# x + alpha * fx on one core: the first load moves from the sync engine's queue to ScalarE's

## The chip, the cores and the metric

The kernel runs on one core of one Trainium2 chip. The metric is the time of one execution on the device in microseconds (us). Before the change the median of three runs is 150.9 us (150.83 to 150.96).

## The reference

Two bfloat16 tensors of shape 512 x 32 x 640 (20.97 MB each) and one bfloat16 scalar go in; one tensor of the same shape comes out.

```python
def reference(x, fx, alpha):
    return x + alpha * fx
```

So 41.94 MB are read from HBM, 20.97 MB are written, and each element needs one multiplication and one addition.

## The kernel before

Each tensor is seen as 128 rows, one for each SBUF partition, of 160 units; a unit (`K`) is 512 elements, or 1 KiB of a row. All data lies in one tile, `room`, of 128 partitions by 207 units (`ROOM`). A written plan, the string `PLAN`, sets the order of all steps, and a loop at the end of the kernel goes through it line by line. The order is kept as written (a manual schedule).

The lines of the plan are:

- `f a b @ at`, `x a b @ at`, `s a b @ at`: one transfer of units a to b of fx, of x or of the output, to or from place `at` of `room`. Each is one `dma_start` in `transfer` (line 96). The row of a transfer is (b - a) KiB long; `f 0 8` has rows of 8 KiB, `f 8 64` rows of 56 KiB, `x 0 64` rows of 64 KiB.
- `a`: `spread_alpha` loads alpha (line 86), and spreads it over the 128 partitions with a matmul against ones (line 90) and a copy to `a_f` (line 91).
- `m t n`: VectorE multiplies n units at place t by alpha, in place (line 110).
- `+ t u n`: VectorE adds the n units at place u to those at place t (line 115).

The plan begins so:

```python
f 0 8 @ 143
f 8 64 @ 151
a
x 0 64 @ 0
m 143 64
f 64 128 @ 79
+ 0 143 24
```

All transfers are issued by the sync engine (SP), on one queue. The first five (`f 0 8`, `f 8 64`, alpha, `x 0 64`, `f 64 128`) wait for nothing and are issued one behind the other at the start. The later loads (`x 64 88`, `x 88 104`, `x 104 128`, `f 128 160`, `x 128 160`) go into places that a multiplication or an addition must have left first, so SP waits for VectorE before it issues them. Then come the stores: `s 0 64` (issued after the addition `+ 192`), `s 64 128` and `s 128 160`. The first multiplication, `m 143 64`, needs both `f 0 8` and `f 8 64`, and alpha. At the end a `nop` on SP waits for all but the last store (line 122). ScalarE has no work of the kernel's at all.

Of the kernel before, what the change touches and what calls it, by code (L numbers as in the profile page):

```python
# [1 line left out]

# [4 lines left out]

ALU = mybir.AluOpType
F32 = mybir.dt.float32

K = 512
P = 128
ROOM = 207

PLAN = """
f 0 8 @ 143
f 8 64 @ 151
a
x 0 64 @ 0
# [3 lines that stand above are left out]
x 64 88 @ 143  # L33
+ 24 167 16
x 88 104 @ 167
+ 40 183 24
x 104 128 @ 183
m 79 64
+ 143 79 17
f 128 160 @ 64  # L40
+ 160 96 7
+ 167 103 16
+ 183 119 9
x 128 160 @ 96
m 64 32
+ 192 128 9
s 0 64 @ 0 after + 192
+ 201 137 6
s 64 128 @ 143
+ 96 64 32  # L50
s 128 160 @ 96
"""


@with_exitstack
def kernel(
    ctx: ExitStack,
    tc: tile.TileContext,
    x: bass.AP,
    fx: bass.AP,  # L60
    alpha: bass.AP,
    out: bass.AP,
):
    nc = tc.nc
    whole = {
        name: t.flatten_outer_dims().rearrange("(p n) d -> p (n d)", p=P)
        for name, t in (("x", x), ("f", fx), ("s", out))
    }
    assert whole["x"].shape[1] == 160 * K

    consts = ctx.enter_context(tc.tile_pool(name="consts", bufs=1))
    psum = ctx.enter_context(tc.tile_pool(name="psum", bufs=1, space=bass.MemoryType.PSUM))
    rooms = ctx.enter_context(tc.tile_pool(name="rooms", bufs=1))
    ctx.enter_context(tc.manual_schedule())

    room = rooms.tile([P, ROOM * K], x.dtype, name="room")
    a_f = consts.tile([P, 1], F32, name="a_f")
    info = mybir.DependencyInfo(mybir.DependencyClass.Sync, mybir.DependencyReason.DATA)
    done, moved = [], {}

    def units(t, a, b):
        return t[:, a * K : b * K]

    def spread_alpha():
        a_1 = consts.tile([1, 1], alpha.dtype, name="a_1")
        done.append(nc.sync.dma_start(out=a_1[:], in_=alpha[None, :]))  # L86
        ones = consts.tile([1, P], alpha.dtype, name="ones")
        nc.vector.memset(ones[:], 1.0)  # L88
        a_ps = psum.tile([P, 1], F32, name="a_ps")
        done.append(nc.tensor.matmul(a_ps[:], ones[:], a_1[:], start=True, stop=True))  # L90
        nc.vector.tensor_copy(out=a_f[:], in_=a_ps[:])  # L91

    def transfer(what, a, b, at, after):
        away, here = units(whole[what], a, b), units(room, at, at + b - a)
        out, in_ = (away, here) if what == "s" else (here, away)
        r = nc.sync.dma_start(out=out, in_=in_)  # L96
        if after:
            tc.add_manual_dep(r.ins, moved[after].ins.name, info, reason="issued late")
        moved[what, a] = r
        done.append(r)  # L100

    for step in PLAN.strip().split("\n"):
        what, *rest = step.split()
        if what == "a":
            spread_alpha()
        elif what == "m":
            t, n = map(int, rest)
            f = units(room, t, t + n)
            done.append(
                nc.vector.tensor_scalar(out=f, in0=f, scalar1=a_f[:], scalar2=None, op0=ALU.mult)  # L110
            )
        elif what == "+":
            t, u, n = map(int, rest)
            xt, f = units(room, t, t + n), units(room, u, u + n)
            moved[what, t] = nc.vector.tensor_tensor(out=xt, in0=xt, in1=f, op=ALU.add)  # L115
            done.append(moved[what, t])
        else:
            a, b, _, at = rest[:4]
            after = (rest[5], int(rest[6])) if len(rest) > 4 else None
            transfer(what, int(a), int(b), int(at), after)  # L120

    last = nc.sync.nop(nofuse=True)
    for i in done[:-1]:
        tc.add_manual_dep(last.ins, i.ins.name, info, reason="all but the last store")


# [1 line left out]
_INS = ['x', 'fx', 'alpha']  # L128
_OUTS = [((512, 32, 640), 'bfloat16')]


# [23 lines left out]
```

## Time and profile before

| quantity | value |
|---|---|
| median of three runs | 150.9 us (150.83 to 150.96) |
| time of the profiled execution | 150.81 us |
| its span | 149.0 us |
| VectorE busy | 65.9 us (44%) |
| DMA queue q1 (all transfers) | 62.92 MB, 98.1% of 16 engines' span |
| mean rate over the span | 422 GB/s |

The span runs from the first to the last instruction that the profiler saw on the core; some 1.8 us of the execution lie outside it. The share of the DMA queue is the time that its packets took, divided by the span of all 16 DMA engines. In this trace a packet of data is one row of a transfer on one DMA engine; each transfer of 128 rows gives each of the 16 engines 8 rows. A window's rate counts a row's bytes where the row begins, so narrow windows swing.

### The profile page before, as it was taken

The numbers are of one execution on the slowest core, as the hardware profiler recorded it, in microseconds if no ns is written. First come the engines' busy times: TensorE is split into PE (matmuls) and PEld (weight loads), VectorE is DVE, ScalarE is ACT, GpSimd is POOL, SyncE is SP. The second block draws the span as 40 slices with busy tenths as digits, with TensorE's granted clock in tenths as the row PEclk, the third lists the DMA queues.
The fourth block names the chain that finished last, engine by engine and source line by source line (L and its number), as shares of the span: only waits on it lengthen the run. The fifth ranks groups of instructions, "written<-read, shape, count | busy, mean of one in ns | idle before, by whom it ended". The sixth has DMA issues, their size and how long they took to land.

```text
span 149.0 us, 85 instructions
## 1 busy us (share of the span) xinstructions
PE 0.2 (0%) x1; PEld 0.1 (0%) x1; DVE 65.9 (44%) x15; POOL 0.2 (0%) x4
## 2 busy tenths in 40 slices
PE   0000000000000000000000000000000000000000
PEld 0000000000000000000000000000000000000000
DVE  0000009940089998699999307969910000000000
POOL 0000000000000000000000000000000000000000
DMA  5997996969899796999998999999696969697994
GB/s 183 592 400 339 493 528 281 563 281 563 369 475 528 317 563 281 416 429 391 462 449 387 422 431 449 449 501 545 299 563 281 563 281 563 281 563 308 457 449 194
DMA packets 1730, 62.92 MB, mean 422 GB/s; under 512 B 194, under 2 KB 194, under 8 KB 194
## 3 DMA queue, kind: packets, MB, share of 16 engines
q1 hardware_dynamic: 1730, 62.92, 98.1%
HBM read 41.94 MB, written 20.97 MB: 422 GB/s over the span
## 4 chain that ended last, share of the span: by engine, by line
DMA 38%; DVE 32%; another core or an unknown queue 1%; SPq 1%; issue 0%; DVEq 0%
DMA room<-in_x_dram 38%; DVE room L115 27%; DVE room L110 6%; SPq L96 1%; SPq L86 0%; DVEq L115 0%
## 5 line engine op out<-in xcount | busy, mean ns | idle before, releaser
L115 DVE TENSOR_TENSOR room<-room 128x12288 bf16<-128x12288 bf16 (+6 forms) x10 | 43.7, 4419 | 11.5 <-DMA room<-in_x_dram 11.5
L110 DVE TENSOR_SCALAR room<-room,a_f 128x32768 bf16<-128x32768 bf16 (+1 forms) x3 | 22.0, 7330 | 9.0 <-DMA room<-in_fx_dram 9.0
L91 DVE COPY a_f<-a_ps 128x1 f32<-128x1 f32 x1 | 0.2, 159 | 21.4 <-PE a_ps L90 21.4
L88 DVE MEMSET ones<- 1x128 bf16 x1 | 0.2, 165 | 0.8 <-PEq L139 0.8
L90 PE MATMUL a_ps<-a,ones 1*128 1x1 bf16 x1 | 0.2, 159 | 22.2 <-DMA a<-in_alpha_dram 22.2
L90 PEld LDWEIGHTS <-ones 1*128 1x128 bf16 x1 | 0.1, 101 | 1.0 <-DVE ones L88 1.0
L139 POOL MEMSET const-bfloat16-1.0<- 128x1 bf16 x1 | 0.1, 101 | 0.0
L139 POOL MEMSET const-uint8-127<- 128x1 uint8 x1 | 0.1, 101 | 0.0
L139 POOL MEMSET const-float32-0.0<- 128x1 f32 x1 | 0.1, 98 | 0.2 <-issue 0.2
L139 POOL MEMSET const-float32-1.0<- 128x1 f32 x1 | 0.1, 98 | 0.0
## 6 DMA issues: line engine op xcount, KB each, us to landing
room<-in_fx_dram SPq DMA_DIRECT2D x1, 7168.0 KB, 21.1
room<-in_x_dram SPq DMA_DIRECT2D x2, 3072.0 KB, 20.7
room<-in_fx_dram SPq DMA_DIRECT2D x1, 4096.0 KB, 15.7
room<-in_x_dram SPq DMA_DIRECT2D x1, 4096.0 KB, 16.7
out_dram<-room SPq DMA_DIRECT2D x1, 4096.0 KB, 39.5
room<-in_x_dram SPq DMA_DIRECT2D x1, 2048.0 KB, 20.5
room<-in_fx_dram SPq DMA_DIRECT2D x1, 1024.0 KB, 4.6
out_dram<-room SPq DMA_DIRECT2D x2, 39.7
```

The costliest lines, as they stand in the source:

```text
L88: nc.vector.memset(ones[:], 1.0)
L90: done.append(nc.tensor.matmul(a_ps[:], ones[:], a_1[:], start=True, stop=True))
L91: nc.vector.tensor_copy(out=a_f[:], in_=a_ps[:])
L96: r = nc.sync.dma_start(out=out, in_=in_)
L110: nc.vector.tensor_scalar(out=f, in0=f, scalar1=a_f[:], scalar2=None, op0=ALU.mult)
L115: moved[what, t] = nc.vector.tensor_tensor(out=xt, in0=xt, in1=f, op=ALU.add)
L139: nc = _bacc.Bacc("TRN2", target_bir_lowering=False, num_devices=1)
```

## The change

The first line of the plan gets the mark `by act`, and `transfer` issues a marked load on `nc.scalar` in place of `nc.sync`. It is still the first transfer in the program's order; place, rows and bytes are the same. On SP the list of transfers then begins with `f 8 64`. The way in which `after` is read is rewritten, and `spread_alpha` takes an argument; on the `a` line that list is empty, so alpha's load gets no wait by it.

```diff
-f 0 8 @ 143
+f 0 8 @ 143 by act
 f 8 64 @ 151
 a
 x 0 64 @ 0
...
-    def spread_alpha():
+    def late(r, after):
+        if after:
+            what, a = after[1], int(after[2])
+            tc.add_manual_dep(r.ins, moved[what, a].ins.name, info, reason="issued late")
+
+    def spread_alpha(after):
         a_1 = consts.tile([1, 1], alpha.dtype, name="a_1")
         done.append(nc.sync.dma_start(out=a_1[:], in_=alpha[None, :]))
+        late(done[-1], after)
...
-        r = nc.sync.dma_start(out=out, in_=in_)
-        if after:
-            tc.add_manual_dep(r.ins, moved[after].ins.name, info, reason="issued late")
+        queue = nc.scalar if after == ["by", "act"] else nc.sync
+        r = queue.dma_start(out=out, in_=in_)
+        if queue is nc.sync:
+            late(r, after)
...
-            spread_alpha()
+            spread_alpha(rest)
...
-            after = (rest[5], int(rest[6])) if len(rest) > 4 else None
-            transfer(what, int(a), int(b), int(at), after)
+            transfer(what, int(a), int(b), int(at), rest[4:])
```

The order of the instructions on PE, VectorE and GpSimd is the same in both programs. ScalarE has one instruction more, the load of `f 0 8`; SP has one fewer, and its other ten data transfers and alpha's stand in the same order.

## The prediction

> **What bounds the kernel now.** I read the page's DMA lines first, then the chain of waits, the waits by engine, and narrow windows at the start and the end.
>
> ```profile
> span 149.0 us, 85 instructions
> HBM read 41.94 MB, written 20.97 MB: 422 GB/s over the span
> q1 hardware_dynamic: 1730, 62.92, 98.1%
> ```
>
> The packets of one queue fill 98.1% of 16 DMA engines. VectorE is busy for 44% only. The page's DMA issues say how the rest of the span splits:
>
> ```profile
> room<-in_fx_dram SPq DMA_DIRECT2D x1, 7168.0 KB, 21.1
> out_dram<-room SPq DMA_DIRECT2D x1, 4096.0 KB, 39.5
> room<-in_fx_dram SPq DMA_DIRECT2D x1, 1024.0 KB, 4.6
> ```
>
> The last number is us from issue to landing. `f 0 8` (1024 KB) is issued at 0.72 us and lands at 5.3. `f 8 64` is issued at 1.16 and lands at 22.26. The last store is issued at 108.78 and lands at 148.28. Between 22.26 and 148.28, 126.0 us, all that is left moves: 62.92 - 8.39 = 54.53 MB, which is 433 GB/s. `x 0 64` (8.39 MB, 19.36 us at that rate) is issued at 1.99, takes 39.6 us and lands at 41.6, 19.3 us behind `f 8 64`: the same rate. So from 22 us on there is no hole in the transfers that the issue times could close. The first 8.39 MB land at 22.26 instead of 19.36: 2.9 us of start. The end holds 0.74 us of drains behind the last landing (148.28 to 149.02), and 150.81 - 149.0 = 1.8 us lie outside the span.
>
> The start in the chain of waits (start, us, what):
>
> ```profile
> 0.72 0.38 SPq L96
> 1.10 0.06 issue
> 1.16 0.42 SPq L96
> 1.58 0.05 issue
> 1.63 0.32 SPq L86
> 1.94 0.04 issue
> 1.99 39.62 DMA room<-in_x_dram
> ```
>
> An issue on SP takes 0.32 to 0.42 us here, and the moved one holds SP from 0.72 to 1.16. Windows (time, engines, clock, DMA share, GB/s):
>
> ```profile
> 1.60:1.70 0.10, 0.00 (x0) 0.00 (x0) 0.00 (x0) 0.00 (x0) 1.00 0.00 0
> 1.70:1.80 0.10, 0.00 (x0) 0.00 (x0) 0.00 (x0) 0.00 (x0) 1.00 2.66 573
> 2.10:2.20 0.10, 0.00 (x0) 0.00 (x0) 0.00 (x0) 0.00 (x0) 1.00 0.00 0
> ```
>
> The first rows begin 1.0 us after the first issue begins. By 2.1 us 16 rows have begun (573, 492, 82 and 164 GB/s over 0.1 us each are 131 kB). From 1.7 to 3.0 the thirteen windows add up to 369 kB, or 45 rows; at 433 GB/s it would be 563 kB. The slow start so costs 194 kB, about 0.45 us. From 3.0 to 4.4 the windows average 422 GB/s: 8 KiB rows run 2.6% below the 433 of the long rows.
>
> ```profile
> DVE room L115 <- DMA room<-in_x_dram: 11.5, 2, 10.3
> DVE room L110 <- DMA room<-in_fx_dram: 9.0, 2, 7.1
> ```
>
> VectorE's longest wait is the 10.3 us between the first multiplication (22.61 to 31.36) and the landing of `x 0 64`. That is the slack of everything the multiplication needs.
>
> **The change part by part.** The sum is made against the profiled execution, 150.81 us, which lies 0.09 below the median; a difference found is put on the median, 150.9.
>
> *Removed from SP:* one issue, 0.72 to 1.16, 0.44 us. `f 8 64` moves up to about 0.72, alpha to 1.19, `x 0 64` to 1.55, `f 64 128` to 1.94. Worth nothing at the end: now, `f 8 64` is issued at 1.16, and by the 1.0 us just read its rows can begin at about 2.2, while `f 0 8` (2.4 us of rows from 1.7, and 0.45 of slow start) occupies the engines until some 4.6. This cover of 2.4 us hides the issue. Without it the 0.44 us would count once. Later loads wait for VectorE or room, not for SP's issues.
>
> *Added on ScalarE:* one issue. The trace shows no issue on ScalarE; the nearest rows are SP's, 0.32 to 0.48 us. Its queue has nothing ahead of it and nothing behind it but the final drain, so nobody waits for ScalarE. Both engines leave the opening barrier almost together (the event rows of L139 stand at 0.6 us for both), so the issue should begin at about 0.72 as well, with data at 1.7. Bounds: if it comes later, SP's `f 8 64` brings the engines 7.34 MB, 16.9 us of rows, and the first data still begin at 1.7, so zero. If its way from issue to first row were shorter than SP's, the gain is at most the 1.0 us of that way; if it takes longer, zero by the cover just named. I take zero, since the nearest row is SP's own.
>
> The Trainium skill, DMA: Bandwidth & Descriptors, section "Latency and other measured facts", gives a first byte of about 0.6 us for transfers from these two queues. By it the data would begin near 1.3 us, and an issue that reached it would bring 0.4 us; the empty window 1.60 to 1.70 contradicts it for SP, and no row shows ScalarE.
>
> *Moved: the order of rows.* `f 0 8` and `f 8 64` are now in two queues at once, on the same bytes per engine: 8 rows of 8 KiB and 8 of 56 KiB. In whichever order they are served, the two together take 8.39 MB at 433 GB/s and the start, and end at about 22.2. If the queues take turns, `f 0 8` lands near 20 us and not at 5.3. The multiplication waits for `f 8 64` in any case. Alpha's two bytes stay behind `f 8 64` on SP's queue; PE received them at 22.22. A delay of either up to 10.3 us ends in VectorE's wait for `x 0 64`; above that it would hold up the additions of L115, and with them the issue of `x 64 88`. Zero.
>
> *The price of alternating two queues* has no row. Lower bound: a gain of the whole slow start, 0.45 us, if the second queue's rows fill its holes. Upper bound: the pair running at the 422 GB/s of short rows rather than 433 for 8.39 MB, 19.88 instead of 19.36 us, a loss of 0.5 us. I take zero, nearest to the long rows, since 7 of 8 bytes of this stretch are still theirs.
>
> *The end:* the same stores on the same queue, and the same final wait. ScalarE's drains are 8 ns each in the rows of L150. Zero.
>
> Sum: 0 us, 150.81 for such an execution, 150.9 for the median.
>
> **The rivals.** About 0.2% (0.3 us) is what a measurement of this kernel can tell from no change.
>
> *Start fills up (faster).* Two queues have rows ready for an engine from the start, so its first slow rows overlap. Price: up to 0.45 us, time 150.45. For it: the window 2.10 to 2.20 in which no row begins. Against: the wait for the first bytes is the same for both queues. It counts from two thirds of the slow start on.
>
> *ScalarE's first row comes earlier (faster).* If data begin 0.4 us sooner on all engines, everything behind moves up by 0.4: 150.5. For it: nothing but that ScalarE is unmeasured. Against: the shared barrier, and SP's 1.0 us. The first-byte figure of the Trainium skill quoted above would allow it. The same page's section "Issuing engines are not separate DMA queues" says that a second issuer saves issue time only; here that is the 0.44 us which the trace shows as covered.
>
> *Two issues get in each other's way at the start (slower).* Now one issue fills the engines one after another: the first 16 rows begin over 1.7 to 2.1, as long as the issue itself takes. If two issues at 0.72 are served in turns, the last engine gets its first row as much later as the second issue takes, 0.38 to 0.42 us; the kernel ends with its slowest engine, so 151.3. It decides from an extra delay of 0.3 us on the last engine. For it: the equal lengths of issue and stagger. Against: a delayed engine could begin with either transfer's rows.
>
> *Alternating costs rate (slower).* The upper bound above, +0.5 us: 151.4. For it: each 56 KiB row would be followed by a short one. Against: there are only 16 such seams for an engine.
>
> *The change does not do what it says:* ScalarE issues late, and SP's queue alone starts the engines. Then the time is that of the forecast.
>
> **How the numbers follow.** No change within 0.3 us: 0.50 (0.02 of it for the late issue). The start fills up 0.12, ScalarE earlier 0.08: faster 0.20. In each other's way 0.17, alternating 0.13: slower 0.30. The predicted time is the likeliest case's, 150.9; its own range is 150.6 to 151.2. Eight in ten must reach into both other sides: down to 150.45, up to 151.4, each widened by the spread of the runs (0.05 to 0.1): 150.4 to 151.5.
>
> **What would show it.** Right: SP's first issue at 0.72 is the 7168 KB one, ScalarE's stands beside it, the first rows begin at 1.7, `f 0 8` lands near 20 us, `f 8 64` near 22.2, `x 0 64` near 41.6, the last store near 148.3. The first two rivals would move all of these landings up together by 0.3 us or more, the other two down; the window in which the first rows begin, and the count of rows by 3.0 us, tell the start from the alternating, which would show only between 3 and 22 us. I am wrong if the landings agree with before within 0.1 us and the time still moves (something outside the span), or if `x 0 64` lands with `f 8 64`'s old distance broken.

## The result, and the profile after

The changed kernel takes 151.47 us (median of 6 runs, 151.31 to 151.67); the kernel before, run beside it, 150.89 us (150.72 to 151.00). The ratio is 1.004, with a 95% interval of 1.0027 to 1.0053: slower by 0.58 us. The forecast was no change.

The page of the changed kernel:

```profile
span 149.7 us, 85 instructions
HBM read 41.94 MB, written 20.97 MB: 420 GB/s over the span
q1 hardware_dynamic: 1586, 61.87, 96.2%
q10 hardware_dynamic: 144, 1.05, 1.7%
```

The span is 0.7 us longer for the same bytes; q10 is the queue of ScalarE with the 1.05 MB of `f 0 8`. The issues say where the time is (KB, then us from issue to landing):

```profile
room<-in_fx_dram SPq DMA_DIRECT2D x1, 7168.0 KB, 22.3
room<-in_fx_dram ACTq DMA_DIRECT2D x1, 1024.0 KB, 22.4
out_dram<-room SPq DMA_DIRECT2D x1, 4096.0 KB, 39.5
```

Both issues begin at 0.73 us. `f 8 64` lands at 23.03 (before: 22.26) and `f 0 8` at 23.1 (before: 5.3). The last store is issued at 109.45 and lands at 148.95. From the landing of `f 8 64` to that of the last store it is 125.9 us, and before it was 126.0. So the whole loss lies ahead of 23 us, and all else is only moved by it. The chain of waits shows the same (start, us, what):

```profile
0.73 0.38 SPq L104
1.11 0.06 issue
1.16 0.31 SPq L92
1.48 0.05 issue
1.53 40.83 DMA room<-in_x_dram
```

SP's issues moved up as forecast: `x 0 64` goes out at 1.53 and not at 1.99. Yet it lands at 42.36, which is 0.75 us later than before.

What happens in the first microseconds stands in the windows. A row's bytes are counted where the row begins, so a window's last column tells how many rows begin in it. First the kernel before, then the changed one:

```profile
1.70:2.10 0.40, 0.00 (x0) 0.00 (x0) 0.00 (x0) 0.00 (x0) 1.00 1.65 328
2.10:2.60 0.50, 0.00 (x0) 0.00 (x0) 0.00 (x0) 0.00 (x0) 1.00 0.62 213
2.60:4.40 1.80, 0.00 (x0) 0.00 (x0) 0.00 (x0) 0.00 (x0) 1.00 0.97 400
```

```profile
1.70:2.10 0.40, 0.00 (x0) 0.00 (x0) 0.00 (x0) 0.00 (x0) 1.00 5.90 1864
2.10:2.60 0.50, 0.00 (x0) 0.00 (x0) 0.00 (x0) 0.00 (x0) 1.00 0.93 344
2.60:4.40 1.80, 0.00 (x0) 0.00 (x0) 0.00 (x0) 0.00 (x0) 1.00 0.00 0
4.40:4.80 0.40, 0.00 (x0) 0.00 (x0) 0.00 (x0) 0.00 (x0) 1.00 1.81 778
4.80:5.40 0.60, 0.00 (x0) 0.00 (x0) 0.00 (x0) 0.00 (x0) 1.00 1.98 847
```

Before, 131 kB of rows begin by 2.1 us: 16 rows of 8 KiB, one for each engine. After, it is 746 kB, which is 13 rows of 56 KiB, and by 2.6 us all 16: the engines began with SP's long rows, not with ScalarE's short ones. Then for 1.8 us no row begins anywhere, since every engine is in its first long row. By the trace's packet records these first rows last 2.28 to 3.52 us, 2.83 in the mean; each 56 KiB row after them lasts 2.12. From there on, long and short rows alternate on every engine, with 2.11 us from the start of a long row to the next short one and 0.31 from the short to the next long, as the two kinds had it before. The last engine begins its first row of x at 22.64 us; before, at 21.90. That is 0.74 us of loss on the slowest engine, and the store that ends the kernel waits for the slowest (the two profiled executions lie 0.65 us apart, the medians 0.58). In the mean over the engines x begins only 0.35 us later, at 22.04 and not at 21.69. So about half of the loss is that the engines are slower at the start, and the rest that they are less even: they begin x over 1.0 us (21.65 to 22.64), where before it was 0.4 (21.49 to 21.90).

### The profile page after: what moved, and what is told of

The parts are those of the page before. It is cut to its first block, busy times and chain, and to the rows that moved or that the text cites. A ratio compares the mean times of both kernels' runs of the same rounds, so it can differ in the third digit from the quotient of the medians.

```text
span 149.7 us, 85 instructions
## 1 busy us (share of the span) xinstructions
PE 0.2 (0%) x1; PEld 0.1 (0%) x1; DVE 65.9 (44%) x15; POOL 0.2 (0%) x4
## 3 DMA queue, kind: packets, MB, share of 16 engines
q10 hardware_dynamic: 144, 1.05, 1.7%
## 4 chain that ended last, share of the span: by engine, by line
DMA 38%; DVE 32%; another core or an unknown queue 1%; SPq 0%; issue 0%; DVEq 0%
DMA room<-in_x_dram 38%; DVE room L123 26%; DVE room L118 6%; SPq L104 0%; SPq L92 0%; DVEq L123 0%
## 6 DMA issues: line engine op xcount, KB each, us to landing
room<-in_x_dram SPq DMA_DIRECT2D x1, 2048.0 KB, 20.5
room<-in_fx_dram ACTq DMA_DIRECT2D x1, 1024.0 KB, 22.4
```

## The experiments

Twelve kernels were run, each beside the kernel before on the same chip. Unless it is said otherwise, the edit is to the first lines of the plan in the changed kernel, and every transfer without `by act` is on SP's queue. Durations of single rows are from the trace's packet records of the one profiled execution. These records do not name the engine of a row; which rows follow each other on an engine is inferred from a row's beginning where another ends.

**Is it the second queue, or the row that the engines begin with?** Four kernels part the two.

Long rows first, one queue:

```diff
-f 0 8 @ 143 by act
 f 8 64 @ 151
+f 0 8 @ 143
```

> Both pieces on SP's queue, the 56 KiB rows first, then the 8 KiB rows; ScalarE issues nothing. Theory A (first row): what costs 0.6 us in the changed kernel is that all 16 engines begin with a 56 KiB row in place of an 8 KiB one, whichever queue it comes from. It expects about 151.5 us, and first rows that last 2.8 us in the mean where later ones last 2.1. Theory B (two queues): what costs is that two issues, or two queues, are served at the same time. It expects 150.9 us, as before the change, and first long rows stretched by no more than the 0.45 us of the slow start before.

Measured: 151.35 us, ratio to before 1.0038 (1.0024 to 1.0052). The windows of this run:

```profile
1.70:2.10 0.40, 0.00 (x0) 0.00 (x0) 0.00 (x0) 0.00 (x0) 1.00 6.65 2150
2.60:4.40 1.80, 0.00 (x0) 0.00 (x0) 0.00 (x0) 0.00 (x0) 1.00 0.00 0
```

It is the picture of the changed kernel without any second queue. The first rows last 2.83 us in the mean.

One piece of 64 KiB rows:

```diff
-f 0 8 @ 143 by act
-f 8 64 @ 151
+f 0 64 @ 143
```

> The first load of fx in one piece of 64 KiB rows on SP's queue. Theory A (first row) expects about 151.5 us, or a little more than with 56 KiB rows first. Theory B (two queues) expects 150.9 us.

Measured: 151.43 us, ratio 1.0036 (1.0024 to 1.0048). First rows last 3.17 us in the mean; later 64 KiB rows last 2.42.

Two queues, short rows first in both:

```diff
 f 0 8 @ 143 by act
-f 8 64 @ 151
+f 8 16 @ 151
+f 16 64 @ 159
```

> As in the changed kernel, the first 8 KiB rows go by ScalarE; but SP's queue too begins with 8 KiB rows (units 8 to 16), and the 48 KiB rows of units 16 to 64 follow. So two queues are used at once and every engine begins with a short row. Theory A (first row) expects 150.9 us. Theory B (two queues) expects about 151.5 us.

Measured: 150.93 us, ratio 1.0007 (0.9999 to 1.0016). Its issues (KB, us from issue to landing):

```profile
room<-in_fx_dram ACTq DMA_DIRECT2D x1, 1024.0 KB, 7.3
room<-in_fx_dram SPq DMA_DIRECT2D x1, 1024.0 KB, 7.2
```

The issues at 0.73 from two engines, and the alternation of two queues (both 1024 KB loads land 7.2 to 7.3 us after their issue), cost nothing that shows. Theory B falls: with one queue the loss is there, with two it is not.

The queues exchanged:

```diff
-f 0 8 @ 143 by act
-f 8 64 @ 151
+f 0 8 @ 143
+f 8 64 @ 151 by act
```

> The two pieces change queues: 8 KiB rows on SP, 56 KiB rows on ScalarE, both issued at once. In the changed kernel every engine began with SP's row. Theory A (first row) expects 150.9 us if SP's rows come first again, and 151.5 us if ScalarE's long rows do, with engines between where they are mixed. Theory B (two queues) expects about 151.5 us in either case.

Measured: 151.40 us, ratio 1.0035 (1.0023 to 1.0047). Its windows:

```profile
1.70:2.10 0.40, 0.00 (x0) 0.00 (x0) 0.00 (x0) 0.00 (x0) 1.00 2.04 328
2.10:3.20 1.10, 0.00 (x0) 0.00 (x0) 0.00 (x0) 0.00 (x0) 1.00 2.14 834
3.20:4.60 1.40, 0.00 (x0) 0.00 (x0) 0.00 (x0) 0.00 (x0) 1.00 0.00 0
```

Every engine did begin with a short row (131 kB by 2.1 us, as before), and still it is slow: theory A as I had put it, on the first row alone, falls too. What the engines took second was ScalarE's long row, begun between 2.1 and 3.2 us. So the theory had to be: long rows cost when they begin inside the slow start. The stretch is here shared by both kinds: the first short rows last 0.82 us in the mean (before: 0.66), the first long rows 2.35 (later ones 2.12), and most of that is in the six that begin before 2.5 us (2.43 to 3.01).

**How short, and for how long?** Four kernels with one queue and another first piece: `f 0 n` and then `f n 64`.

```diff
-f 0 8 @ 143 by act
-f 8 64 @ 151
+f 0 2 @ 143
+f 2 64 @ 145
```

> All on SP: units 0 to 2 of fx first (2 KiB rows), then units 2 to 64 (62 KiB rows). By the row rates seen, eight 2 KiB rows pass an engine in some 0.6 us, so the long rows begin while the slow start of 1.7 to 3.0 us is still on. Theory A1 (the first row alone counts) expects 150.9 us. Theory A2 (long rows must stay out of the whole slow start) expects 151.2 to 151.5 us.

Measured with 2 KiB rows first: 151.14 us, ratio 1.0020 (1.0011 to 1.0029). The long rows begin at 2.4 to 3.1 us and last 2.77 in the mean; later 62 KiB rows last 2.34. The same edit with 4:

> All on SP: units 0 to 4 of fx first (4 KiB rows), then units 4 to 64 (60 KiB rows). Eight 4 KiB rows would pass an engine in some 1.3 us, so the long rows begin at about 3.2 to 3.6 us, between those of the run with 2 KiB rows first (2.4 to 3.1 us, stretched by 0.5 us in the mean) and those of the kernel before (4.6 to 5.0, not stretched). The theory that only long rows within the slow start cost expects 150.9 to 151.0 us, and long rows stretched by less than 0.2 us. If it were the length of the first row alone that counts, 4 KiB should be no better than 2 KiB: 151.1 us.

Measured with 4 KiB rows first: 150.83 us, ratio 1.0001 (0.9993 to 1.0010). The long rows begin at 3.3 to 4.2 us and last 2.29 in the mean; later ones last 2.27. The profile is of one of the three slower runs of its eleven (151.16 us; the other two took 151.07 and 151.28, the rest at most 150.90). Its long rows are hardly stretched; what is late is a few engines whose short rows took longer (up to 1.01 us), and the last engine comes to x at 22.36. So in this execution an uneven start cost time without long rows in it. Again with 16:

> All on SP: units 0 to 16 of fx first (16 KiB rows), then units 16 to 64 (48 KiB rows). Theory C (the longer the rows at the start, the more it costs, since engines that are served first hold the reads longer) expects a value between that of 8 KiB rows and that of 56 KiB rows, 151.0 to 151.2 us. A threshold above 16 KiB would give 150.9.

Measured: 150.88 us, ratio 1.0004 (0.9995 to 1.0013), below what was expected of a cost that grows evenly. And with 32:

> All on SP: units 0 to 32 of fx first (32 KiB rows), then units 32 to 64 (32 KiB rows). If the cost grows with the length of the rows in the slow start, this lies between 16 KiB (150.88 us) and 56 KiB (151.35 us): about 151.1. If there is a threshold between 16 and 32 KiB, 151.35; if above 32 KiB, 150.9.

Measured: 151.22 us, ratio 1.0025 (1.0015 to 1.0036). Both a step between 16 and 32 KiB and a growing cost fit this interval; which it is, these runs do not tell.

By first row, then, in us: 2 KiB 151.14, 4 KiB 150.83, 8 KiB 150.86, 16 KiB 150.88, 32 KiB 151.22, 56 KiB 151.35, 64 KiB 151.43. Each is a median, beside 150.83 to 150.86 for the kernel before in the same rounds (8 KiB is that kernel). Too short a row, 2 KiB, costs because the long rows come too early behind it: they begin at 2.4 to 3.1 us and are stretched.

**Why do long rows at the start cost?** Three kernels.

Other addresses:

```diff
-f 0 8 @ 143 by act
-f 8 64 @ 151
+f 8 64 @ 151 pitch
+f 0 8 @ 143
...
+        if after == ["pitch"]:
+            flat = fx.flatten_outer_dims().rearrange("r d -> (r d)")
+            in_ = flat[: P * 30080].rearrange("(p n) -> p n", p=P)[:, : (b - a) * K]
+            after = []
```

> 56 KiB rows first on SP, as in the run with the long rows first; but this transfer reads its rows from HBM at a distance of 60160 bytes and not 163840, so it fetches other data of fx and the product of these units is not the reference's. Theory D (at the start all engines read at the same offset of rows 160 KiB apart, in lockstep, and collide in HBM) expects the stretch of the first long rows to shrink and the time to fall towards 150.9 us. Theory C (long rows at the start, whatever their addresses) expects 151.35 us and a mean first row of 2.8 us again.

Measured: 151.23 us, ratio 1.0029 (1.0017 to 1.0040), first rows 2.86 us in the mean. A pitch of 160 KiB is not what costs; with 60160 bytes the rows are stretched as much. Other pitches were not tried.

A short first use, then a wait:

```diff
-f 0 8 @ 143 by act
-f 8 64 @ 151
+f 0 1 @ 143
+f 1 64 @ 144 after f 0
```

> All on SP: units 0 to 1 of fx (1 KiB rows, 8 for each engine) first, and only when they have landed are the long rows (63 KiB) issued. The wait itself costs some 2 us of idle transfers. Theory W (the slow start is a first use of queue, engines or memory that short rows take the cost of) expects the first long rows to last about as long as later ones, 2.33 us. Theory C (16 engines begin long rows together) expects them stretched by some 0.7 us in the mean, as when they are first.

Measured: 153.03 us (two runs), of which some 2.1 us are the wait (the long rows begin at 3.8 and not at 1.7). The 0.13 MB moved ahead of the wait are worth 0.3 us at 433 GB/s, so of the 2.2 us above the kernel before an estimated 0.4 are left for the second start. The windows of its second start:

```profile
3.80:4.30 0.50, 0.00 (x0) 0.00 (x0) 0.00 (x0) 0.00 (x0) 1.00 6.30 2064
4.30:6.40 2.10, 0.00 (x0) 0.00 (x0) 0.00 (x0) 0.00 (x0) 1.00 0.00 0
```

All 16 long rows begin by 4.3 us (1.03 MB) and no next row begins by 6.4. They last 2.6 to 3.8 us, 3.15 in the mean; later 63 KiB rows last 2.38 (the 2.33 of my expectation was a little low), so the stretch is 0.77 us. So it is not a first use of the queue or of the engines. It came back when all engines, after a pause, began long rows together.

The packet or the share of a partition:

```diff
-f 0 8 @ 143 by act
-f 8 64 @ 151
+f 0 64 @ 143 pieces
...
+        if after == ["pieces"]:
+            in_ = units(whole[what], 0, 128).rearrange("p (c two e) -> p c two e", c=4, two=2)[:, :, 0, :]
+            out = here.rearrange("p (c e) -> p c e", c=4)
+            after = []
```

> The first load of fx in one transfer of 64 KiB for each partition, as in the unsplit run, but read as four runs of 16 KiB that lie 32 KiB apart in HBM, so that each 64 KiB row is moved in four packets; it fetches other data of fx, and the product of these units is not the reference's. If the length of one packet is what counts, it behaves as the run with 16 KiB rows first: 150.9 to 151.0 us, no packet of 64 KiB stretched by 0.8 us, and the engines reach x within 0.5 us of each other. If the size of the transfer or of a partition's share counts, 151.4 us as unsplit.

Measured: 151.25 us, ratio 1.0031 (1.0019 to 1.0043). That is clear of 150.9 to 151.0, and its interval takes in the 151.4 of the unsplit load. But the first packets last 1.26 us in the mean, near the 1.17 of the run with 16 KiB rows first. And this form of transfer also brings its first data 0.13 us later in the mean than that run, and 16 packets more for each engine. The last engine comes to x at 22.36 us, between the 22.09 of the run with 16 KiB rows first and the 22.70 of the unsplit one. Packet, size and the later first data can't be parted here, so this run decides nothing.

**The changed kernel with two lines exchanged.** Alpha's load goes ahead of the long rows on SP's queue:

```diff
 f 0 8 @ 143 by act
-f 8 64 @ 151
 a
+f 8 64 @ 151
```

> The changed kernel with alpha's load ahead of the 56 KiB rows on SP's queue. ScalarE's issue of the 8 KiB rows stands at 0.73 us, and the long rows are issued about 0.4 us later, as in the kernel before; but they lie in another queue than the short ones, so an engine can take a long row after its first or second short one, at 2.2 to 2.9 us. If long rows within the slow start cost, whichever row is first: 151.1 to 151.4 us. If only the very first row of an engine counts: 150.9 us.

Measured: 150.82 us, ratio to before 0.9996 (0.9987 to 1.0006), with the second queue in use. The profile shows why, and that my picture of the queues was wrong. Its issues, and its windows:

```profile
room<-in_fx_dram SPq DMA_DIRECT2D x1, 7168.0 KB, 21.2
room<-in_fx_dram ACTq DMA_DIRECT2D x1, 1024.0 KB, 4.5
```

```profile
2.60:4.40 1.80, 0.00 (x0) 0.00 (x0) 0.00 (x0) 0.00 (x0) 1.00 0.96 391
4.40:4.80 0.40, 0.00 (x0) 0.00 (x0) 0.00 (x0) 0.00 (x0) 1.00 4.27 1802
```

`f 0 8` lands 4.5 us after its issue and not 22.4: the engines took all eight of ScalarE's short rows before any of SP's long ones, though the long ones were issued at 1.13 us. The long rows begin at 4.6 to 4.9 us, as in the kernel before, and last 2.15 us in the mean. The premise of my expectation, that a long row would follow the first or second short one, was not met, so the run does not part the two cases that it names. It does show that a second queue with short rows ahead of the long ones takes the time of the kernel before. What put the short rows first, the 0.4 us between the two issues or alpha's load standing ahead on SP's queue, this one kernel does not tell.

## Why the prediction was wrong

**The bound** was read rightly: the transfers set the end, and from 23 us on nothing changed but the place in time (125.9 against 126.0 us between the same two landings).

**The issue removed from SP** was worth nothing, as forecast: SP's loads went out 0.4 to 0.5 us earlier and landed later.

**The issue added on ScalarE** is where the sum first failed. It begins at 0.73 us as expected. But the prediction said that SP's rows could stand in for ScalarE's at no cost ("if it comes later, SP's `f 8 64` brings the engines 7.34 MB"), because first data begin at 1.7 us either way. They did begin at 1.7, but with long rows, and first data of 56 KiB rows are dearer than first data of 8 KiB rows.

**The order of rows**, a term put at zero, holds the same mistake in the open: "In whichever order they are served, the two together take 8.39 MB at 433 GB/s and the start, and end at about 22.2." I had measured the slow start (0.45 us) and treated it as fixed. It depends on what the engines begin with: 0.74 us later on the slowest engine in the changed kernel, and the same loss within the intervals in a kernel with one queue. In the kernel before, the 8 KiB first piece is what runs during the slow start. The change took that from it, since SP's queue then began with the long rows. The sum's zero for this term measured 0.58 us between the medians. The sign that the prediction gave, `f 0 8` landing near 20 us if the queues take turns, failed too (23.1). With the queues exchanged its rows had all been moved by 20.5 us, and it still landed at 22.9: its completion writes (packets of 4 bytes in the records) went out at 21.6 to 22.6, behind the last long row of the other queue.

**The rivals.** "In each other's way at the start" had the right sign, place and nearly the right size (0.38 to 0.42 us forecast, 0.58 measured), but not the mechanism: two issues at once cost nothing that shows when both bring short rows (1.0007), and SP's issues alone cost as much when the long rows come first (1.0038). That the wide range (150.4 to 151.5) reaches 151.47 at all is luck, since its upper end was set by the price of alternating. "Alternating costs rate" is refuted by the row periods, which did not change from 3 to 22 us. The two faster rivals did not happen: the start became slower, and the first row came at 1.7 us from ScalarE's queue too, where it was first (the run with alpha ahead).

The Trainium skill, DMA: Bandwidth & Descriptors, section "Queues, rings and completion order", says that an engine goes round the queues that have work, packet by packet, with typically some 9 to 17 descriptors in a packet. In the changed kernel the turns are of single rows: one long row, one short row. In the run with alpha ahead they are not: all eight short rows of an engine went first. If such a packet is one row, the rule fits only the first of the two kernels, and if it is an engine's whole share of a transfer, only the second; which it is, no run here shows. Its section "Issuing engines are not separate DMA queues", which I had quoted against a gain, held: the saved issue time was covered, and nothing else was won. The first-byte figure of about 0.6 us of the Trainium skill, DMA: Bandwidth & Descriptors, section "Latency and other measured facts", which the prediction holds against the empty window before 1.7 us, was counted there from the begin of the issue. Counted from its end (0.72 + 0.38 = 1.10), the first rows at 1.73 us come 0.63 us later, so the trace does not contradict it.

**What stays open** is why SP's row is the first on every engine when both issues begin at 0.73 us, and why 16 engines that begin long rows together are slower and less even than 16 that begin short ones. The pitch of the addresses is excluded for the one other value tried, and a first use of the queue and the engines by the run with the wait. That the engines served first read far ahead into long rows while the others wait would fit the spread of 2.28 to 3.52 us, but it is only argued. So is the length of the packet as against the size of the share.

## What to carry to other kernels

Where a kernel is bound by its transfers from the first microsecond, as this one is, let the first rows of all DMA engines be short ones (4 to 16 KiB here), and enough of them that no long row begins before the start is over (3.3 us here, 1.6 us after the first data). Splitting the first load does that only while the short piece stands ahead of the long one: on one queue the order of issue keeps it; on two queues with both issues at once it was lost, and it was kept in the one kernel that issued the long piece 0.4 us later, behind another load. Before moving an issue to another queue, ask what becomes the first row of the queue that it leaves.

## What the runs showed of the hardware

- Two loads issued from SP and ScalarE at 0.73 us alternate row by row on every engine, with SP's row first in each of the two profiles with rows of different length (56 KiB in the changed kernel, 8 KiB with the queues exchanged). With the issues at 0.73 and 1.13 us, and alpha's load ahead of the later one, the earlier load's eight rows went first without any alternation.
- The first long rows of engines that stood idle are stretched by 0.71 us in the mean at 56 KiB and 0.77 us at 63 KiB, again after 2 us of use and a pause; 8 KiB rows first lose about 0.45 us in all.
- The kernel's end follows the latest engine, not the mean. In 13 of the 14 profiles the span ends 127.0 to 127.1 us after the last engine has begun x (127.6 in the run with 32 KiB rows first, whose profile is of its slowest execution, 151.80 us), while counted from the mean of the engines it is 127.2 to 127.7. So the stretch of the first row is not by itself the cost: 16 KiB rows first last 1.17 us and later 0.62, yet the last engine comes to x at 22.09 us, and no loss of time shows (1.0004).
